# Float32r matmuls of a linear-attention and FFN kernel that read and write their columns in woven blocks of 16, from the halves' ends on

## The chip, the core and the metric

The kernel runs on one core of a Trainium2 chip. The metric is the device time of one launch in microseconds (us); the tables of the trace use nanoseconds (ns) where they say so. The engines are called by the profile's names: PE is TensorE's matmul row, PEld its weight loads, DVE is VectorE, ACT is ScalarE, POOL is GpSimd, SP is the engine whose queue issues the DMAs.

## What is computed

Linear attention without softmax (8 batches, 8 heads, 576 positions, 64 values a head), a root-mean-square norm a head, and a two-layer FFN with SiLU over the 4608 tokens (512 to 2048 to 512), all in float32 accuracy:

```python
kv  = einsum('bhsd,bhse->bhde', k, v)
out = einsum('bhsd,bhde->bhse', q, kv)
out = out / sqrt(mean(out * out, axis=-1, keepdims=True) + 1e-06) * g_norm
x   = out.transpose(0, 2, 1, 3).reshape(B * S, H * D)      # 4608 x 512
h   = x @ w_in                                             # 512 -> 2048
y   = (h / (1 + exp(-h))) @ w_out                          # 2048 -> 512
```

## The kernel before

The tokens are cut into 9 tiles of 512 (t = 0 to 8), the 2048 hidden values into 16 blocks of 128 (f). Every float32 operand of the FFN is kept as two float32r parts, an upper and a lower one, and each product is made of three matmuls (lower by upper, upper by lower, upper by upper) that add into one bank of PSUM. A matmul has a stationary operand of 128 x 128, loaded by a weight load of its own (a LDWEIGHTS for each MATMUL), and a moving operand of 128 partitions by 256 or 512 columns that is read from SBUF while the products are written to PSUM.

Three places make nearly all of TensorE's work:

- `products` (L474), for t = 0 and 1: h of one f, 4 row blocks of x by 3 matmuls, 512 columns each. The stationary side is `wi`, the moving side is `x` (t = 0: the tiles `x0` to `x3`; t = 1: `x_place`).
- `product` (L634), from t = 2 on: h of two f at once by a seven-product scheme. `pair_step` calls it seven times with 6 matmuls of 256 columns each, so 42 a pair step. The moving side lies in `x_operands` (a view of `x_place`) or in `operand4` to `operand6`, the stationary side is `wi` or one of the sums of `wi` blocks, which are read back from DRAM in each pair step (`load_sums`).
- `project` (L505), for all t: y += g @ w_out. The stationary side is a 128-column piece of `gh` or `gl` (the two parts of the SiLU's result), the moving side is a row block of `wo` with 512 columns; 12 matmuls for each f, so 24 a pair step. In the last tile one of the four banks is cut into two halves of 256 columns.

A tile from t = 2 on has 8 pair steps, 56 in all. The attention of later batches (L253 for kv, L288 to L290 for q by kv, 288 columns) is spread between these by hand-written tables of jobs, a few batches ahead of its use. The order on each engine is the order of the code (`manual_schedule`); nothing is reordered by a scheduler.

The SBUF addresses follow from the order of the `const.tile` and pool calls. `SHIFT` (48 columns of 4 bytes) moves `x_operands` inside `x_place` and with it the tiles behind. In the built program, with addresses taken modulo 256 bytes, the tiles `wi`, `wo`, `gh`, `gl` and `x3` start at 224; so does the second tile's x (t = 1). `x0` to `x2`, `x_operands` and `operand4` to `operand6` start at 160, 64 bytes before the weights' place. All starts are thus half a block off a grid of 64 bytes.

Of the kernel before, what the change touches and what calls it, by code (L numbers as in the profile page):

```python
# [8 lines left out]
F32 = mybir.dt.float32  # L9
# [21 lines left out]
def linear_attention_rms_silu_ffn(  # L31
# [22 lines left out]
    nc = tc.nc  # L54
    B, NP, P, S = q.shape
# [3 lines left out]
    TN = 512  # L59
# [5 lines left out]
    const = ctx.enter_context(tc.tile_pool(name="const", bufs=1))  # L65
# [13 lines left out]
        nc.gpsimd.memset(t, 0.0)  # L79
    ident = const.tile([P, P], F32, name="ident", tag="kh", bufs=2)  # L80
    make_identity(nc, ident)
    warm_up = const.tile([P, 1], F32, name="warm_up")
    nc.gpsimd.memset(warm_up, 1.0)
    gcol = const.tile([P, 1], F32, name="gcol")
    both = const.tile([P, P], F32, name="both", tag="kl", bufs=2)
    nc.gpsimd.tensor_copy(out=both, in_=ident)
    for i in range(4):
        nc.gpsimd.tensor_copy(
            out=both[32 * i:32 * i + 32, 32 * (i ^ 1):32 * (i ^ 1) + 32], in_=ident[32 * i:32 * i + 32, 32 * i:32 * i + 32]
        )  # L90
    d_eps = const.tile([P, 1], F32, name="d_eps")
    nc.gpsimd.memset(d_eps, float(D) * EPS)

    def load_g():
        for h in range(P // D):
            nc.sync.dma_start(out=gcol[h * D:(h + 1) * D, :], in_=g_norm.rearrange("(d o) -> d o", o=1))
# [6 lines left out]

    SHIFT = 48
    x_place = const.tile([P, NP * 2 * TN + SHIFT], F32R, name="x_place")
    x_second = x_place[:, :NP * 2 * TN].rearrange("p (c a n) -> p c a n", c=NP, a=2)
    x_operands = x_place[:, SHIFT:].rearrange("p (c a k n) -> p c a k n", c=NP, a=2, k=2)  # L110
    x_first, lates = {}, {}

    def spare(n, shape, dtype, name):
        return const.tile(shape, dtype, name=name, tag=f"spare{n}")

    def late(n, shape, dtype, name):
        if not lates:
            const.tile([P, 64 - SHIFT], F32, name="gap")
        if name not in lates:
            lates[name] = const.tile(shape, dtype, name=name, tag=f"late{n}")  # L120
        return lates[name]

    def x32(c, w):

        return late(c // 2, [P, 2, TN], F32, f"x32_{c // 2}")[:, c % 2, w]
# [14 lines left out]
    def full_tile(kind, f):  # L140
        if kind == "wo":
            t = late(1, [P, 2, NP * P], F32, "wo_full")[:, f % 2]
        else:
            t = tmp.tile([P, S], F32, name="full", tag="tmp")[:, :NP * P]
        fulls[kind, f] = t
        return t
# [54 lines left out]
    def x_part(t, a, c):  # L201

        if t == 1:
            return x_second[:, c, a]
        if c not in x_first:
            kind = {"shape": [P, 2, TN], "dtype": F32R, "name": f"x{c}"}
            x_first[c] = spare(c, **kind) if c < 3 else late(0, **kind)
        return x_first[c][:, a]
# [245 lines left out]
        return calls + 3 * newton(y, u, m)  # L454


    def h_bank():
        return ps_h.tile([P, 512], F32, name="hp", tag="h")

# [10 lines left out]
    def products(hp, t, f, c):  # L470
        w = parts["wi", f]
        fs = slice(c * P, (c + 1) * P)
        for i, (a, b) in enumerate(((0, 1), (1, 0), (0, 0))):
            nc.tensor.matmul(  # L474
                out=hp[:, :TN], lhsT=w[:, a, fs], rhs=x_part(t, b, c),
                start=(c == 0 and i == 0), stop=(c == NP - 1 and i == 2),
            )

# [20 lines left out]
    def project(t, f, gh, gl, bank, n, cs):  # L499
        first, last = order(t)[0], order(t)[-1]  # L500
        w = parts["wo", f]
        ns = slice(n * P, (n + 1) * P)
        bank = bank[:, :cs.stop - cs.start]
        for i, (g, a) in enumerate(((gh, 1), (gh, 0), (gl, 0))):
            nc.tensor.matmul(  # L505
                out=bank, lhsT=g[:, ns], rhs=w[:, a, cs], start=(f == first and i == 0), stop=(f == last and i == 2)
            )
        if f == last:
            ob = tmp.tile([P, S], F32, name="ob", tag="tmp")[:, :cs.stop - cs.start]
            (nc.scalar.copy if n % 2 else nc.vector.tensor_copy)(out=ob, in_=bank)  # L510
            nc.sync.dma_start(out=out[t * TN + n * P:t * TN + (n + 1) * P, cs], in_=ob)
# [9 lines left out]
    def order(t):  # L521

        if t < 2:
            return [(f + t * HF) % NF for f in range(NF)]
        return [f for i in range(HF) for f in (i + HF, i)]
# [69 lines left out]
    def operand(j):  # L595

        if j < 4:
            return x_operands[:, j]
        if j not in operands:
            operands[j] = spare(j - 4, [P, 2, 2, H], F32R, f"operand{j}")  # L600
        return operands[j]
# [26 lines left out]
    def product(m, i, out):  # L628
        j, _, a_of = seven[m]
        x = operand(j)  # L630
        n = 0
        for c in range(2):
            for a, b in ((0, 1), (1, 0), (0, 0)):
                nc.tensor.matmul(  # L634
                    out=out, lhsT=a_of(i, a, c), rhs=x[:, b, c], start=(n == 0), stop=(n == 5)
                )
                n += 1

# [10 lines left out]
    def pair_step(t, i, groups):  # L649
# [5 lines left out]
        def due(n):  # L655
            while n > 0 and groups:
                n -= (groups[0][-1].stop - groups[0][-1].start) / DM
                project(*groups.pop(0))
# [9 lines left out]

        begin(g)
        bank, other = h_bank(), h_bank()  # L670
        u, v = bank[:, :H], bank[:, H:]
        y, z = other[:, :H], other[:, H:]
# [6 lines left out]
        if g == 2 * NF:  # L679
            due(4)  # L680
        product(1, i, u)
        product(2, i, v)
        product(6, i, y)
        product(7, i, z)
        nc.scalar.copy(out=p1, in_=u)  # L685
# [117 lines left out]
    with tc.manual_schedule():  # L803

        first = [FirstPair(c) for c in range(NP)]
        stats = at_bank().rearrange("p (c i j) -> p c i j", i=2, j=8)
        second = plan(1, 3)
        for item in ORDER.split():
            kind, n = item.rstrip("0123456789"), int(item.lstrip("wiopbg") or 0)
# [6 lines left out]
            else:  # L816
                load_block(kind, n)

        idle, kv_bank = h_bank(), h_bank()

        def keep_warm(n, bank=idle):
# [18 lines left out]
        def warm_products(c, *fs):  # L840
            if not warm:
                warm.extend([h_bank(), acc_bank()])
            for f in fs:
                products(warm[f], 0, f, c)
# [115 lines left out]
        for t in range(NT):  # L960
# [7 lines left out]
            for step, f in enumerate(order(t)):  # L968
                g = t * NF + step
                for job in first_jobs.pop(g, ()):  # L970
                    job()
                for item in prepped:
                    split_block(*item, nc.scalar.copy)
                prepped = []
                if t == 0:
                    prepped = [("wi", f + 2)] * (3 <= f + 2 < NF) + [("wo", f)] * (f > 0)
                run(sum((bits(*item) for item in prepped), []), *[call() for call in chains.pop(g, ())])
                if t == 0 and 3 < f + 3 < NF:
                    magnitude("wi", f + 3)
                if t == 0 and f < WARM:  # L980
                    hp = warm[f]
                    products(hp, t, f, NP - 1)
                else:
                    hp = h_bank()
                    for c in range(NP):
                        products(hp, t, f, c)
                pend.append(((t, f, *gate(t, hp)), sums))
                if t == 0 and f + 1 < NF:
                    magnitude("wo", f + 1)
                for job in mid_jobs.pop(g, ()):  # L990
                    job()
                if len(pend) > LAG:
                    item, olds = pend.pop(0)
                    for old in olds:
                        project(*item, *old)
                for job in last_jobs.pop(g, ()):
                    job()
# [4 lines left out]
        for old in sums:  # L1002
            for item, _ in pend:
                project(*item, *old)
# [41 lines left out]
```

## Time and profile before

| | us |
|---|---|
| median of 3 runs (839.11 to 839.32) | 839.13 |
| the profiled execution, own time | 839.63 |
| its span, first to last instruction | 837.8 |
| PE busy in the span | 826.8 (99%) |
| DVE busy | 528.9 (63%) |
| ACT busy | 359.0 (43%) |
| POOL busy | 145.9 (17%) |
| queue of the DMAs, share of 16 engines | 42.4% |

The busy time of PE counts matmuls whose ends are modelled and overlap, so a mean duration (389 ns for 512 columns) is longer than the step from one start to the next. The step is read from the chain of work that ended last: there a piece such as `PE acc L505 x24` with its length gives the time that 24 matmuls in a row took on the path.

### The profile page before, as it was taken

Reading aid. Unit: us, or ns where it says so; the run is one execution under the profiler, and the core shown is the slowest. Engines: PE = TensorE matmul, PEld = TensorE weight load, DVE = VectorE, ACT = ScalarE, POOL = GpSimd, SP = SyncE. Lnnn points to the kernel's source line nnn. Section 1 sums busy time; section 2 is a strip of 40 time slices with the busy share of each in tenths; the row PEclk is TensorE's granted clock in tenths of the full one; section 3 lists DMA queues with packets and bytes.
Section 4 is the critical chain, followed back from the end, with each engine's and each line's share of the span. In section 5 each row is a group of like instructions: output and inputs, shape, how many; then the busy total and the mean of one; then the engine's idle time right before and its main releaser. Section 6 shows DMA issues by size and latency. Waiting matters only on the chain.

```text
span 837.8 us, 14032 instructions
## 1 busy us (share of the span) xinstructions
PE 826.8 (99%) x5454; PEld 734.6 (88%) x5454; DVE 528.9 (63%) x1027; ACT 359.0 (43%) x744; POOL 145.9 (17%) x142
## 2 busy tenths in 40 slices
PE   8999999999999999999999999999999999999998
PEld 7767888888899999998999998999999999999997
DVE  4886875788476567657766667656865664464332
ACT  3766564534453245325532355225532432243222
POOL 2786983423010002000200011001100000000000
PEclk9999999999999999999999999999999999999999
DMA  8879011337343634364424452444423343334331
GB/s 322 313 257 362 4 57 51 136 145 261 122 161 100 215 115 146 101 214 144 165 91 160 163 173 88 158 158 157 151 84 103 106 155 103 105 102 151 100 102 51
DMA packets 42418, 122.55 MB, mean 146 GB/s; under 512 B 4848, under 2 KB 5104, under 8 KB 42352
## 3 DMA queue, kind: packets, MB, share of 16 engines
q1 hardware_dynamic: 42352, 121.65, 42.4%
q8 instruction: 43, 0.70, 0.4%
q14 instruction: 23, 0.19, 0.1%
HBM read 103.81 MB, written 17.83 MB: 145 GB/s over the span
## 4 chain that ended last, share of the span: by engine, by line
PE 94%; DMA 4%; POOL 1%; ACT 0%; issue 0%; SPq 0%
PE acc L505 46%; PE hp L634 33%; PE hp L474 9%; PE at L253 2%; DMA k<-in_k 1%; DMA wo<-in_moe_w_out 1%; DMA early_wi<-in_v 1%; DMA v<-in_v 1%; PE at L289 1%; PE at L288 1%; PE at L290 1%; PE at L505 1%; DMA wi<-in_moe_w_in 1%; PE at L286 1%; POOL wo L191 0%
## 5 line engine op out<-in xcount | busy, mean ns | idle before, releaser
L505 PE MATMUL acc<-wo,gh 128*128 128x512 f32 (+1 forms) x1152 | 354.1, 389 | 0.1
L505 PEld LDWEIGHTS acc<-wo,gh 128*128 128x128 f32 x1152 | 210.3, 188 | 39.7 <-POOL wo L191 0.3
L505 PE MATMUL acc<-wo,gl 128*128 128x512 f32 x576 | 223.0, 387 | 0.5 <-POOL gl L485 0.5
L634 PE MATMUL hp<-x_place,wi 128*128 128x256 f32 x1344 | 167.8, 280 | 0.0
L634 PEld LDWEIGHTS hp<-x_place,wi 128*128 128x128 f32 x1344 | 162.0, 189 | 0.0
L634 PEld LDWEIGHTS hp<-operand,wi 128*128 128x128 f32 x1008 | 126.0, 189 | 3.9
L505 PEld LDWEIGHTS acc<-wo,gl 128*128 128x128 f32 x576 | 108.1, 188 | 23.5 <-POOL gl L485 0.9
L634 PE MATMUL hp<-operand,wi 128*128 128x256 f32 x1008 | 127.5, 281 | 0.0
L275 POOL TENSOR_TENSOR ql<-q,qh 128x576 fp32r<-128x576 f32 x24 | 35.6, 1483 | 376.0 <-ACT qh L274 341.9
L685 ACT COPY wi<-hp 128x256 f32<-128x256 f32 x56 | 20.9, 373 | 140.9 <-PE hp L634 140.9
L643 ACT ACTIVATE gh<-gf 128x512 fp32r<-128x512 f32 x56 | 35.4, 633 | 94.4 <-DVE gf L698 81.6
L643 ACT ACTIVATE gh<-wi 128x512 fp32r<-128x512 f32 x56 | 35.5, 634 | 79.8 <-DVE wi L698 68.0
L686 DVE TENSOR_TENSOR gf<-hp,wi 128x256 f32<-128x256 f32 x28 | 11.9, 425 | 84.8 <-ACT wi L685 84.8
L686 DVE TENSOR_TENSOR wi<-hp,wi 128x256 f32<-128x256 f32 x28 | 11.9, 424 | 84.3 <-ACT wi L685 84.3
L474 PE MATMUL hp<-x,wi 128*128 128x512 f32 x180 | 46.4, 402 | 1.4 <-POOL wi L191 1.4
L474 PE MATMUL hp<-x_place,wi 128*128 128x512 f32 x192 | 46.4, 390 | 0.0
L647 DVE TENSOR_TENSOR gl<-wi,gh 128x512 fp32r<-128x512 f32 x56 | 38.4, 685 | 11.4 <-ACT wi L644 11.4
L687 DVE TENSOR_TENSOR wi<-hp,wi 128x256 f32<-128x256 f32 x56 | 23.8, 425 | 32.3 <-PE hp L634 32.3
L647 DVE TENSOR_TENSOR gl<-gf,gh 128x512 fp32r<-128x512 f32 x56 | 39.0, 696 | 7.3 <-ACT gf L644 7.3
L294 ACT ACTIVATE sq<-at 128x288 f32<-128x288 f32 x56 | 22.9, 410 | 45.6 <-PE at L290 38.9
L474 PEld LDWEIGHTS hp<-x_place,wi 128*128 128x128 f32 x192 | 35.7, 188 | 7.3
L316 DVE SCALAR_TENSOR_TENSOR x<-o,gcol,yT 128x128 f32<-128x128 f32 (+7 forms) x52 | 40.7, 784 | 1.9
(142 smaller groups left out, 1006.8 us busy)
## 6 DMA issues: line engine op xcount, KB each, us to landing
wi<-sums_in_dram SPq DMA_DIRECT2D x112, 512.0 KB, 3.3
out<-ob SPq DMA_DIRECT2D x35, 256.0 KB, 2.4
wi<-in_moe_w_in SPq DMA_DIRECT2D x16, 512.0 KB, 7.8
wo<-in_moe_w_out SPq DMA_DIRECT2D x16, 512.0 KB, 8.9
sums_in_dram<-sum_parts SPq DMA_DIRECT2D x16, 512.0 KB, 2.6
k<-in_k SPq DMA_DIRECT2D x28, 288.0 KB, 5.2
v<-in_v SPq DMA_DIRECT2D x28, 288.0 KB, 5.4
q<-in_q SPq DMA_DIRECT2D x28, 288.0 KB, 4.0
```

The source lines that it names most:

```text
L253: nc.tensor.matmul(out=self.kv[h], lhsT=self.k[rows, c, :], rhs=self.v[rows, c, :], start=(start and r == 0), stop=(stop and r == 4),)
L275: nc.gpsimd.tensor_tensor(out=self.ql, in0=self.q, in1=self.qh.bitcast(F32), op=ALU.subtract)
L294: nc.scalar.activation(out=self.sq[:, self.w], in_=self.ps, func=AF.Square)
L316: nc.vector.scalar_tensor_tensor(out=to, in0=self.o[:, a:e], scalar=gcol, in1=self.yT, op0=ALU.mult, op1=ALU.mult)
L474: nc.tensor.matmul(out=hp[:, :TN], lhsT=w[:, a, fs], rhs=x_part(t, b, c), start=(c == 0 and i == 0), stop=(c == NP - 1 and i == 2),)
L505: nc.tensor.matmul(out=bank, lhsT=g[:, ns], rhs=w[:, a, cs], start=(f == first and i == 0), stop=(f == last and i == 2))
L634: nc.tensor.matmul(out=out, lhsT=a_of(i, a, c), rhs=x[:, b, c], start=(n == 0), stop=(n == 5))
L643: nc.scalar.activation(out=gh, in_=x, func=AF.Silu)
L647: nc.vector.tensor_tensor(out=gl, in0=x, in1=gh.bitcast(F32), op=ALU.subtract)
L685: nc.scalar.copy(out=p1, in_=u)
L686: nc.vector.tensor_tensor(out=c1[:, low], in0=v, in1=p1, op=ALU.add)
L687: nc.vector.tensor_tensor(out=u2, in0=y, in1=p1, op=ALU.add)
```

## The change

The three functions named above pass their moving operand and their output through a new view, `woven`. It cuts the columns into two halves and each half into blocks of 16 columns. The blocks are taken in this order: the last block of the first half, the last block of the second half, the block before it of the first half, and so on down to the halves' first blocks; inside a block the columns still ascend. Moving side and output go through the same view, so each column's result lands where it did, and nothing that reads PSUM or writes the operands changes. The stationary operands, their weight loads, the number of matmuls and their columns are as before. The 288-column matmuls of the attention and the small float32 ones are not woven.

Three placements go with it. `SHIFT` falls from 48 to 32 columns. `warm_up` and `gcol` are allocated behind `both` in place of ahead of it, and a tile of 8 columns named `gap` is added ahead of `x_place`. In the built program `wi`, `wo`, `gh`, `gl`, `x3` and the x of t = 1 then start at 0 modulo 256 bytes, and `x0` to `x2`, `x_operands` and the operands at 128: every start lies on a grid of 64 bytes, so that a block of 16 columns is one block of the grid.

```diff
-    warm_up = const.tile([P, 1], F32, name="warm_up")
-    nc.gpsimd.memset(warm_up, 1.0)
-    gcol = const.tile([P, 1], F32, name="gcol")
     both = const.tile([P, P], F32, name="both", tag="kl", bufs=2)
...
+    warm_up = const.tile([P, 1], F32, name="warm_up")
+    nc.gpsimd.memset(warm_up, 1.0)
+    gcol = const.tile([P, 1], F32, name="gcol")
     d_eps = const.tile([P, 1], F32, name="d_eps")
     nc.gpsimd.memset(d_eps, float(D) * EPS)
+    const.tile([P, 8], F32, name="gap")
...
-    SHIFT = 48
+    SHIFT = 32
...
-            const.tile([P, 64 - SHIFT], F32, name="gap")
+            const.tile([P, 64 - SHIFT], F32, name="gap2")
...
+    def woven(t):
+
+
+        return t.rearrange("p (h k e) -> p k h e", h=2, e=16)[:, ::-1]
+
...
-                out=hp[:, :TN], lhsT=w[:, a, fs], rhs=x_part(t, b, c),
+                out=woven(hp[:, :TN]), lhsT=w[:, a, fs], rhs=woven(x_part(t, b, c)),
...
-                out=bank, lhsT=g[:, ns], rhs=w[:, a, cs], start=(f == first and i == 0), stop=(f == last and i == 2)
+                out=woven(bank), lhsT=g[:, ns], rhs=woven(w[:, a, cs]), start=(f == first and i == 0), stop=(f == last and i == 2)
...
-                    out=out, lhsT=a_of(i, a, c), rhs=x[:, b, c], start=(n == 0), stop=(n == 5)
+                    out=woven(out), lhsT=a_of(i, a, c), rhs=woven(x[:, b, c]), start=(n == 0), stop=(n == 5)
```

No engine's order of instructions changes, only the form of these matmuls. On PE, in a pair step of the first tiles of the seven-product scheme, where `product` (six matmuls a row) is followed by `project`, there stood before (the numbers tell buffers of one tile apart):

```order
L634 MATMUL hp<-operand_2216,wi_2185 128x256 x6
L634 MATMUL hp<-x_place,wi_2185 128x256 x6
L634 MATMUL hp<-x_place,wi_1104 128x256 x6
L634 MATMUL hp<-x_place,wi_2187 128x256 x12
L505 MATMUL acc<-wo_1174,gh 128x512 x2
L505 MATMUL acc<-wo_1174,gl 128x512
```

and in the changed program, at the same place:

```order
L641 MATMUL hp<-operand_2217,wi_2186 128x8x2x16 x6
L641 MATMUL hp<-x_place,wi_2186 128x8x2x16 x6
L641 MATMUL hp<-x_place,wi_1105 128x8x2x16 x6
L641 MATMUL hp<-x_place,wi_2188 128x8x2x16 x12
L512 MATMUL acc<-wo_1175,gh 128x16x2x16 x2
L512 MATMUL acc<-wo_1175,gl 128x16x2x16
```

The rows stand one for one; 256 columns have become 8 times 2 blocks of 16, and 512 have become 16 times 2, so a matmul now reads and writes 16 or 32 short runs.

## Rows read from the trace of the kernel before

**Rows 1.** The profile's page: span, PE's busy time, PE's granted clock in 40 slices.

```profile
span 837.8 us, 14032 instructions
PE 826.8 (99%) x5454; PEld 734.6 (88%) x5454; DVE 528.9 (63%) x1027; ACT 359.0 (43%) x744; POOL 145.9 (17%) x142
PEclk9999999999999999999999999999999999999999
```

**Rows 2.** The chain of waits over the whole span: its shares by line.

```profile
by line: PE acc L505 45.9%; PE hp L634 32.9%; PE hp L474 9.3%; PE at L253 2.2%; DMA k<-in_k 1.0%; DMA wo<-in_moe_w_out 1.0%; DMA early_wi<-in_v 0.9%; DMA v<-in_v 0.8%; PE at L289 0.8%; PE at L288 0.8%; PE at L290 0.8%; PE at L505 0.7%; DMA 
```

**Rows 3.** What PE waited for, seven rows in all: us in total, times, longest.

```profile
PE hp L824 <- POOL ident masks.py:199: 2.0, 1, 2.0
...
PE acc L505 <- POOL gl L485: 0.5, 1, 0.5
```

**Rows 4.** The chain of waits, a pair step of t = 3: start, length (us), piece.

```profile
343.35 4.95 PE hp L634 x42
348.30 5.44 PE acc L505 x24
```

**Rows 5.** The chain of waits in t = 0: two plain float32 matmuls of 288 columns.

```profile
81.22 0.48 PE at L286 x2
```

**Rows 6.** The chain of waits, a stretch with attention matmuls between: start, length, piece.

```profile
411.66 0.13 PE at L290
411.79 2.06 PE hp L634 x18
...
414.26 2.09 PE acc L505 x9
```

**Rows 7.** The chain of waits, t = 0 (first two) and t = 1 (last two).

```profile
84.47 2.79 PE hp L474 x12
87.26 2.73 PE acc L505 x12
...
173.20 2.72 PE hp L474 x12
175.92 2.72 PE acc L505 x12
```

**Rows 8.** The chain of waits, a pair step of the last tile.

```profile
767.12 4.78 PE hp L634 x42
771.90 2.41 PE acc L505 x12
774.31 0.36 PE at L505 x3
```

**Rows 9.** PE's groups by line and shape: count, then busy time and mean of one.

```profile
L505 PE MATMUL acc<-wo,gh 128*128 128x512 f32 x1120 | 347.8, 392 | 0.1
L505 PE MATMUL acc<-wo,gl 128*128 128x512 f32 x560 | 218.5, 390 | 0.5 <-POOL gl L485 0.5
L634 PE MATMUL hp<-x_place,wi 128*128 128x256 f32 x1344 | 167.8, 280 | 0.0
L634 PE MATMUL hp<-operand,wi 128*128 128x256 f32 x1008 | 127.5, 281 | 0.0
L474 PE MATMUL hp<-x_place,wi 128*128 128x512 f32 x192 | 46.4, 390 | 0.0
L474 PE MATMUL hp<-x,wi 128*128 128x512 f32 x180 | 46.4, 402 | 1.4 <-POOL wi L191 1.4
```

**Rows 10.** PE's timeline near the start: start, length, group of matmuls.

```profile
13.95 1.06 PE L341 MATMUL acc<-kvm,early_wi 128*128 128x128 f32 x8
14.84 0.39 PE L824 MATMUL hp<-ident 128*128 128x128 f32 x2
```

**Rows 11.** Stretch, length, busy of PE, PEld, DVE, ACT, POOL; PEclk, DMA, GB/s.

```profile
20.00:120.00 100.00, 95.17 (x555) 75.54 (x555) 79.21 (x131) 63.36 (x128) 78.94 (x79) 1.00 0.53 200
...
400.00:500.00 100.00, 100.00 (x703) 91.02 (x702) 65.50 (x135) 43.45 (x93) 8.96 (x6) 1.00 0.45 151
```

## The prediction

> **What bounds the kernel now.** I read the page first. Its first part says that PE is busy for 826.8 of 837.8 us, and the row of the granted clock says that the throttle never took anything: 2.4 GHz, the higher of the two levels, in all 40 slices [rows 1]. The chain of waits agrees: lines 505, 634 and 474, the three matmuls of the FFN, hold 45.9%, 32.9% and 9.3% of the span [rows 2]. PE's own waits are seven, 2.0 us the longest and 0.5 the shortest [rows 3], under 14 us together whatever lies between. So the time is the number of matmuls times the step from one to the next, and an edit that leaves the order and every other engine alone can only act on that step.
>
> The step is what the reader should look at next, and the chain shows it without the modelled ends. In a quiet pair step 42 matmuls of 256 columns take 4.95 us, 117.9 ns each, and 24 of 512 take 5.44 us, 226.7 ns each [rows 4]. At 2.4 GHz and one column a clock these would be 106.7 and 213.3 ns, so 11.2 and 13.4 ns are lost in each. That one clock a column is the natural rate is seen from the plain float32 matmul: 288 columns take 0.24 us, which is exactly two clocks a column and nothing beside [rows 5]; the loss belongs to the full-rate stream.
>
> Now the same forms elsewhere. Right behind attention matmuls 18 of the 256-column kind take 2.06 us, 114.4 each, while nine of 512 take 2.09 us, 232.2 each [rows 6]. In t = 0, line 474 takes 2.79 us for 12, 232.5 each, with line 505 behind it at 227.5; in t = 1 the same line 474 takes 2.72, 226.7 each [rows 7]. In the last tile the 42 take 4.78 us, 113.8 each [rows 8]. Same line, same columns, same clock, no wait: the step has at least two values for each form. What differs between t = 0 and t = 1 in line 474 is where the moving tile starts against the weights (160 against 224 modulo 256 bytes, then 224 against 224), beside busier neighbours. My reading is that the moving stream and the next weight load, which run side by side, get in each other's way in SBUF, that each encounter costs some clocks, and that the start addresses and what went before decide how many there are.
>
> **The change part by part.** *Orders, counts, other engines.* The counts stay: 2352 matmuls of 256 columns in line 634, 1680 of 512 in line 505, and 372 in line 474 [rows 9], with 96 halves of 256 in line 505 beside. Outputs land where they did, so no reader of PSUM moves. The two tiles allocated later and the 8-column gap cost nothing.
>
> *The weave.* A straight stream walks up through its tile; woven, it stays on one block's place (modulo the halves' distance) for two blocks and walks down at half the speed. If the weight load also walks from its last column down, at half the moving stream's pace, the two keep their distance through the whole load and stop meeting. Whether the load does that is shown by no row. What the rows give is bounds. For 256 columns: at worst nothing is won, 117.2 ns on average (32.9% of 837.8 is 275.6 us over 2352); at best the bare columns, 106.7. Between lies a row with a weight load for each matmul and no straight full-rate stream beside it: eight plain float32 matmuls of 128 columns in 0.89 us (13.95 to 14.84), 111.3 ns each [rows 10]. The load of 128 columns therefore fits into 111.3 ns, and I take 111.3 as the woven step, since this is the nearest row with a load in every step. For 512 columns: most steps are the quiet 226.7 [rows 4, 7], some are 227.5 or 232.2 [rows 6, 7]; I take 227.1 as the mean. Best 213.3. A load takes at most half of such a matmul, so more of the loss should go, but no row shows a 512 below 226.7; I take the middle of 226.7 and 213.3, 220.0.
>
> *The sum.* Line 634: 2352 x 5.9 ns = 13.9 us. Line 505: 1680 x 7.1 = 11.9 us, and the 96 halves, at 120 ns (0.36 us for 3 [rows 8]), brought to about 114, 0.6 us. Line 474: t = 1, 192 x 6.7 = 1.3 us; t = 0, 180 x 12.5 = 2.3 us. Together 30.0 us. In t = 0 the cover is thin: DVE, ACT and POOL are busy 79, 63 and 79 of 100 us [rows 11], so of what lines 474 and 505 win there (2.3 and 192 x 7.5 = 1.4 us) I give half back to waits on POOL, 1.9 us. From t = 2 on nothing is near: DVE at 65.5 of 100 us, DMA at 0.45 of its share [rows 11]; four percent less PE time raises that to 68, and PE waits for nothing there. So 28.1 us.
>
> *Alignment.* Every start moves by 32 bytes or so, for weights and for the 144 unwoven 288-column matmuls too. Their step is 0.13 or 0.14 us [rows 6]; a change of 5 ns either way is 0.7 us. I take nothing.
>
> The Trainium skill speaks against the reading: "TensorE: Matmul & The Clock Gate", in its Part 2, gives PE two independent SBUF read ports, so that the next weights' load takes nothing from the running matmul. By that rule the weave would change nothing; [rows 4, 6, 7], with two steps for one form, do not settle it, since a neighbour's write could also be the cause. The same page's isolated step, columns over 2.4 GHz and about 2.5 ns, would be 109.2 and 215.8 ns here, an estimate from that page by which the sum would be some 19 us for line 634 and 19 for line 505.
>
> **The rivals.** *Only the unlucky phases go.* The weave keeps the streams in the better of the two states that the trace already has: 113.8 ns [rows 8] and 226.7. That is 2352 x 3.4 = 8.0 us, 1680 x 0.4 = 0.7, and 180 x 5.8 = 1.0 in t = 0: 9.7 us, 829.9. For it: no row of 2352 in line 634 shows a group below 113.8. Against: the better states are those of straight streams, in which the two still cross.
>
> *No change.* The loss is not an encounter with the weight load but belongs to the full-rate float32r stream: then 839.6, within 1 us. For it: 226.7 is twice 113.3, so the loss is nearly in proportion to the columns in the better states, as it would be if the stream itself lost one clock in 16, and a load of fixed size would not give that. Against: the other states, which are not in proportion (117.9 and 226.7; 114.4 and 232.2). The rule of the two ports is this rival.
>
> *Slower: each run costs.* A woven matmul reads and writes 16 or 32 runs in place of one, and a jump of address on either side may cost a clock. At one clock of 0.417 ns, 16 runs are 6.7 ns and 32 are 13.3: 2352 x 6.7 + 2052 x 13.3 = 43.0 us. If my gain is there too, the end is 811.5 + 43.0 = 854.5; if not, 882.6. It decides from 0.37 ns a run (5.9 over 16) for 256 columns, and from 0.22 ns (7.1 over 32) for 512: less than one clock. For it: no row of before has a stream with jumps, so nothing bounds it. Against: each run is 64 bytes and now starts on a grid of 64. The Trainium skill's "PSUM — Partial Sum Buffer", under Specifications, says that any non-contiguous access pattern slows matmuls significantly; that rule is this rival. [...]
>
> *More than forecast.* All loss goes: 2352 x 10.5 + 1680 x 13.8 + 192 x 13.4 + 180 x 19.2, 53.9 us, 785.7. I see it as the floor.
>
> **How the numbers follow.** The profiled execution took 839.63 us, 1.8 more than its span; the median is 839.13. 839.6 less 28.1 is 811.5, and on the median's scale 811.0; I predict 811. Chances: forecast and what lies about it (788 to 822) 0.46, only the phases 0.22 (822 to 837), no change 0.10, each run costs 0.20, below 788 0.02. A difference of 0.2%, 1.7 us, is about what a measurement of this kernel can tell from no change; so faster 0.70, same 0.10, slower 0.20. The range runs from 788, near the floor, over the phases and no change to 843, where a run's cost has just passed break-even; what it leaves out is most of the slower case and the floor. The likeliest case by itself is 788 to 822.
>
> **What would show it.** In the chain of waits of the changed kernel the pieces of 42 and of 24 matmuls give the answer: about 4.67 us and 5.28 us for the forecast, 4.78 and 5.44 for the phases alone, 4.95 and 5.44 for no change, over 5.2 and 5.6 for a cost a run. The 12 of line 474 in t = 0 should come down from 2.79 most. Weight loads, counts and granted clock should be as before, and PE's waits beyond t = 0 still absent; were new waits on DVE or ACT to stand in the rows from t = 2 on, my cover would be wrong. If one form gains and the other doesn't, then the relative start of the two streams, which differs between line 505 (0) and line 634 (128 bytes), decides and not the weave alone.

## The result and the profile after

The changed kernel takes 847.14 us (median of 3 runs, 846.99 to 847.26) against 839.13 before: a ratio of 1.0095 with a 95% interval of 1.0072 to 1.0118. It is slower by about 1%, where 811 us was forecast, and outside the range. Its lines 481, 512 and 641 are lines 474, 505 and 634 of before.

The page of the changed kernel, the parts that answer to [rows 1]:

```profile
span 845.2 us, 14053 instructions
PE 835.0 (99%) x5454; PEld 733.5 (87%) x5454; DVE 529.4 (63%) x1027; ACT 359.3 (43%) x744; POOL 145.3 (17%) x142
PEclk9999999999999999999999999999999999999999
```

The same 5454 matmuls, the higher clock level (2.4 GHz) in all 40 slices, the other engines within 0.6 us of before. PE's waits are seven again. The first and the last row of that view (us in total, times, longest):

```profile
PE hp L831 <- POOL ident masks.py:199: 2.0, 1, 2.0
...
PE hp L255 <- DMA early_wo<-in_v: 0.2, 1, 0.2
```

The longest is still 2.0 us, and the seven add up to 7.0 us where they were 7.7, so no wait makes the 8 us. What grew is the step. The chain of waits by line (share of the span), to be held against [rows 2]:

```profile
by line: PE acc L512 46.4%; PE hp L641 32.5%; PE hp L481 9.3%; PE at L255 2.2%; DMA wo<-in_moe_w_out 1.0%; DMA k<-in_k 1.0%; PE at L292 0.8%; PE at L290 0.8%; PE at L291 0.7%; DMA v<-in_v 0.7%; DMA wi<-in_moe_w_in 0.7%; PE at L512 0.7%; DMA
```

Multiplied by the spans, `project` went from 384.5 to 392.2 us, `product` from 275.6 to 274.7, `products` from 77.9 to 78.6: together 7.5, and the span grew by 7.4. (A share is rounded to 0.1%, some 0.4 us either way.) So the whole loss lies in the 512-column matmuls.

The chain in a quiet pair step of t = 4 (start, length in us, piece), to be held against [rows 4]:

```profile
440.86 5.61 PE acc L512 x24
446.46 4.90 PE hp L641 x42
```

24 matmuls of 512 columns take 5.60 us where they took 5.44: 233.3 ns a step in place of 226.7. 42 of 256 columns take 4.90 where they took 4.95: 116.7 in place of 117.9. One form loses 6.6 ns, the other wins 1.2.

The chain elsewhere: t = 0 and t = 1 (to be held against [rows 7]), behind attention matmuls ([rows 6]), and in the last tile ([rows 8]):

```profile
83.84 2.77 PE hp L481 x12
86.61 2.80 PE acc L512 x12
...
173.90 2.80 PE hp L481 x12
...
415.00 2.10 PE hp L641 x18
...
417.49 2.12 PE acc L512 x9
...
773.25 4.90 PE hp L641 x42
```

Line 481 wins 1.7 ns a matmul in t = 0 (2.79 to 2.77 for 12), where three of its four moving tiles start 128 bytes before the weights' place and `x3` at it, and loses 6.6 in t = 1, where both start at the same place modulo 256 bytes (2.72 to 2.80). In the last tile `product` loses what it had: 4.78 becomes 4.90. The woven 256-column step is 116.7 everywhere, quiet or disturbed; the straight one was 117.9, 114.4 or 113.8.

### The profile page after: what moved, and what is told of

Read it like the earlier page. It is cut to its first block, busy times and chain, and to the rows that moved or that the text cites. A ratio compares the mean times of both kernels' runs of the same rounds, so it can differ in the third digit from the quotient of the medians.

```text
span 845.2 us, 14053 instructions
## 1 busy us (share of the span) xinstructions
PE 835.0 (99%) x5454; PEld 733.5 (87%) x5454; DVE 529.4 (63%) x1027; ACT 359.3 (43%) x744; POOL 145.3 (17%) x142
## 4 chain that ended last, share of the span: by engine, by line
PE 94%; DMA 4%; POOL 1%; ACT 0%; issue 0%; SPq 0%
PE acc L512 46%; PE hp L641 32%; PE hp L481 9%; PE at L255 2%; DMA wo<-in_moe_w_out 1%; DMA k<-in_k 1%; PE at L292 1%; PE at L290 1%; PE at L291 1%; DMA v<-in_v 1%; DMA wi<-in_moe_w_in 1%; PE at L512 1%; DMA early_wi<-in_v 1%; PE at L288 1%; POOL wo L193 0%
## 5 line engine op out<-in xcount | busy, mean ns | idle before, releaser
L512 PE MATMUL acc<-wo,gh 128*128 128x512 f32 (+1 forms) x1152 | 359.0, 392 | 0.1
L512 PE MATMUL acc<-wo,gl 128*128 128x512 f32 x576 | 225.5, 391 | 0.5 <-POOL gl L492 0.5
L693 DVE TENSOR_TENSOR wi<-hp,wi 128x256 f32<-128x256 f32 x28 | 11.9, 425 | 87.1 <-ACT wi L692 87.1
L693 DVE TENSOR_TENSOR gf<-hp,wi 128x256 f32<-128x256 f32 x28 | 11.9, 425 | 87.0 <-ACT wi L692 87.0
```

Source lines behind the costliest of these rows:

```text
L512: nc.tensor.matmul(out=woven(bank), lhsT=g[:, ns], rhs=woven(w[:, a, cs]), start=(f == first and i == 0), stop=(f == last and i == 2))
L693: nc.vector.tensor_tensor(out=c1[:, low], in0=v, in1=p1, op=ALU.add)
```

## The experiments

Below, the **distance** is how far the weights' start lies behind the moving operand's start, modulo 256 bytes. Three theories were tried. *Phase*: the step of a matmul with a weight load beside it is set by the distance and by the order in which the moving stream visits its columns. *Placement*: the new start addresses alone do it, and the weave is beside the point. *Each run costs*: a jump of address has a price, whatever the addresses.

### The parts of the change, one by one

**New starts, straight streams.** The changed kernel with

```diff
-        return t.rearrange("p (h k e) -> p k h e", h=2, e=16)[:, ::-1]
+        return t
```

> The new placement (SHIFT 32, the gap tile, all starts on the grid of 64 bytes) with straight columns on both sides, as before. Theory 'phase' (the step is set by how the moving stream and the next weight load meet, and the weave breaks the good meeting of the 512-column matmuls): 512 columns stay at 226 to 227 ns in quiet stretches, the time is 836 to 841 us. Theory 'each run costs' (about 6.6 ns for 32 runs): the same, 839 or a little less. Theory 'placement' (the grid of 64 bytes, not the weave, costs): 847 us, with 512 columns at 233 ns.

Measured: 846.72 us (846.31 to 846.95), ratio 1.0089 [1.0074, 1.0104]. Its chain by line, and a quiet pair step:

```profile
by line: PE acc L512 45.6%; PE hp L641 33.3%; PE hp L481 9.2%; PE at L255 2.2%; DMA wo<-in_moe_w_out 1.0%; DMA wi<-in_moe_w_in 0.9%; DMA k<-in_k 0.9%; PE at L290 0.8%; PE at L291 0.8%; DMA early_wo<-in_k 0.8%; PE at L292 0.8%; PE at L512 0.
...
445.04 5.04 PE hp L641 x42
450.07 5.48 PE acc L512 x24
```

The time is as placement expected, but in the other form; the 836 to 841 of phase missed. `project` stays near its old step (228.3 ns; distance 0 as before), and `product`, whose distance went from 64 to 128 bytes, rises from 117.9 to 120.0. By shares of the span, in us:

| | before | new starts, straight | new starts, woven (the change) |
|---|---|---|---|
| `project` | 384.5 | 385.3 | 392.2 |
| `product` | 275.6 | 281.4 | 274.7 |
| `products` | 77.9 | 77.7 | 78.6 |
| span | 837.8 | 845.0 | 845.2 |

The change is thus two edits: the new starts cost 7.2 us of the span, most of it in `product`; the weave gives 6.7 back there and takes 6.9 in `project`. The split depends on the order: taken first, the weave costs 10.1 us, and the new starts then give 2.1 back, as the next run shows.

**The weave, old starts.** The kernel before, with `woven` and its six uses and nothing else of the diff.

> The weave in all three places, with the placement of before (SHIFT 48, starts 32 bytes off the grid of 64, so each block of 16 columns lies over two blocks of the grid). Theory 'each run costs': 847 us, as after, or more, since a run then touches two blocks. Theory 'phase': some other time, 840 to 870, since the relative starts are others. Theory 'placement': 839.

Measured: 849.23 (849.17 to 849.47), ratio 1.0120 [1.0103, 1.0136]. A quiet pair step:

```profile
441.47 5.60 PE acc L510 x24
447.07 4.94 PE hp L639 x42
```

At distance 0 the woven 512-column step is 233.3 with the old starts too, so half a block off the grid of 64 or on it is the same. At distance 64 the 256-column step gains almost nothing (117.6). The time is far from the 839 of placement; phase (840 to 870) and a cost a run (847 or more) both allow it.

**The weave in `product` alone.** The changed kernel with straight operands in the other two:

```diff
-                out=woven(hp[:, :TN]), lhsT=w[:, a, fs], rhs=woven(x_part(t, b, c)),
+                out=hp[:, :TN], lhsT=w[:, a, fs], rhs=x_part(t, b, c),
...
-                out=woven(bank), lhsT=g[:, ns], rhs=woven(w[:, a, cs]), start=(f == first and i == 0), stop=(f == last and i == 2)
+                out=bank, lhsT=g[:, ns], rhs=w[:, a, cs], start=(f == first and i == 0), stop=(f == last and i == 2)
```

> Of the changed kernel the weave in the 256-column product alone; project and products read and write straight. Theory 'phase': the 512-column matmuls return to 226.7 ns and the 256-column ones stay near 116.6, so about 847 less 2050 x 6 ns, 833 to 836 us. Theory 'each run costs': 256 columns carry 16 runs, so half the cost of a 512; 512 return to 226.7, 836 to 840. Theory 'placement': 847.

Measured: 837.75 (837.64 to 838.03), ratio 0.9984 [0.9975, 0.9993], a gain of 1.4 us.

```profile
441.70 4.90 PE hp L641 x42
446.60 5.44 PE acc L512 x24
```

The good half of the change alone: 116.7 where it was 117.9, and 226.7 kept. Woven columns can be cheaper than straight ones, though 16 runs stand in place of one. The time missed the 833 to 836 of phase and lies in the range of each run costs, so it does not decide between them: the sum took 6 ns from every 512-column matmul, but behind attention matmuls the weave had cost less (nine in 2.12 us, straight 2.09 [rows 6]).

### The step by itself

**Matmuls alone.** A program of nothing but float32r matmuls with a weight load each (the model is left out; a copy of an input to the output runs beside the first three groups): groups of 48 with 512 columns and 72 with 256, at eight distances, 0 to 448 bytes in steps of 64 (names end in a to h).

```diff
+    "long_woven": (512, woven, woven, 0),
+    "long_woven_out": (512, in_turn, woven, 0),
...
+                            out=write(bank[:cols, :n]), lhsT=weights[:, w0:w0 + cols], rhs=read(moving[:, m0:m0 + n]),
```

> Not the model's computation: matmuls alone, in rows of 48 (512 columns) or 72 (256 columns), nothing else running beside, for each way of reading and writing (straight, straight 32 bytes off the grid, woven down, woven up, blocks down without the interleave, woven on the moving side alone, woven on the output side alone) and for eight distances of the weights' start from the moving start (letters a to h: 0 to 448 bytes in steps of 64); 'light' rows load only 32 weight columns; what is written to the output is a copy of an input. Theory 'phase': the step changes with the letter by 4 to 8 ns, for straight and woven alike, the output side alone changes nothing, and light rows come near 213 and 107 ns. Theory 'each run costs': woven is 6 to 7 ns above straight at 512 and about 3 at 256 for every letter, light rows too. No dependence on the letter at all would be against 'phase'.

The chain of waits of that program (start, length of the whole group in us, group); `up` is the weave with ascending blocks, `out` weaves only the output, `light` loads 32 weight columns in place of 128:

```profile
32.44 11.16 PE long_straight_c L96 x48
43.60 10.99 PE long_straight_d L96 x48
54.60 10.90 PE long_straight_e L96 x48
65.50 11.20 PE long_straight_f L96 x48
...
187.34 11.19 PE long_woven_a L96 x48
198.54 11.36 PE long_woven_b L96 x48
209.89 10.96 PE long_woven_c L96 x48
...
276.29 11.52 PE long_woven_up_a L96 x48
...
547.75 10.93 PE long_woven_out_a L96 x48
...
647.40 11.13 PE long_light_b L96 x48
...
821.65 8.48 PE short_straight_b L96 x72
830.13 8.55 PE short_straight_c L96 x72
...
966.65 8.40 PE short_woven_c L96 x72
...
1163.20 8.16 PE short_light_b L96 x72
```

Divided by the counts, in ns:

| distance, bytes | 0 | 64 | 128 | 192 |
|---|---|---|---|---|
| 512 straight | 227.1 | 233.3 | 232.5 | 229.0 |
| 512 woven, descending | 233.1 | 236.7 | 228.3 | 228.3 |
| 512 woven, ascending | 240.0 | 240.0 | 240.0 | 240.0 |
| 256 straight | 120.0 | 117.8 | 118.8 | 117.8 |
| 256 woven, descending | 119.9 | 117.4 | 116.7 | 116.7 |

Distances e to h repeat a to d, so the period is 256 bytes (e stands for a in the straight row of 512, since the program's start lies in a). One form, one clock, nothing else at work from the fourth group on, and the step moves by 6 ns with the distance alone: this shows that *phase* is real. It holds most of the case's numbers: `project` at 0 goes from 227.1 to 233.1, `product` at 64 straight is 117.8, at 128 woven 116.7. One it does not hold: at 128 straight it has 118.8, where the kernel with the new starts took 120.0. Moving all starts by 32 bytes changed no group by more than 0.02 us (the first aside), the output's weave is free (10.93 and 11.20 woven, 10.90 and 11.20 straight) while the moving side's alone gives the woven steps (11.20 and 11.36), and ascending blocks cost the same at every distance. The *placement* theory in its plain form and *each run costs* both fail here: the same 32 runs take 228.3 to 240.0 ns.

With a load of 32 columns the 512-column step is 231.9 at b and 230.4 to 231.9 at all eight distances: nearly no dependence, but not the 213 that was expected. The 256-column step does fall, to 113.3, but not to 107.

**The distance mended in the changed kernel.** A tile that nothing uses moves `gh` and `gl`, the weights of `project`, by 128 bytes:

```diff
+    small.tile([P, 32], F32, name="pad", bufs=1)
```

> The changed kernel with a pad of 128 bytes ahead of gh and gl, so that line 505's stationary tiles start 128 bytes (modulo 256) from wo, as line 634's already do, and not at the same place. Theory 'phase', by the table of matmuls alone (woven 512 at distance 0: 233.3 ns, at 128: 228.3; measured in the changed kernel 233 at distance 0): 1680 x 5 ns = 8 us less than the changed kernel, 839 us, with the 24 of a pair step at 5.48 us instead of 5.60. Theory 'each run costs': no change, 847.

Measured: 839.47 (839.12 to 839.72), ratio 1.0003 [0.9993, 1.0012].

```profile
442.70 4.90 PE hp L642 x42
447.60 5.49 PE acc L513 x24
```

The time is as phase expected. The weave is as it was, every run of it, and 7.7 of the 8.0 us are gone: the woven step of `project` falls from 233.3 to 228.8 (228.3 in the table). This settles that the loss is the weave *at distance 0*.

**The distance spoiled in the kernel before.** The same with 16 columns: `gh` and `gl` come to distance 64, no weave anywhere.

```diff
+    small.tile([P, 16], F32, name="pad", bufs=1)
```

> The kernel of before (straight) with a pad of 64 bytes ahead of gh and gl alone, so line 505 has distance 64 where it had 0. Theory 'phase', by the table (straight 512: 226.7 at 0, 233.4 at 64): 1680 x 6.7 ns less the few stretches that are disturbed already, 9 to 11 us more, 848 to 850. Theory that only the order of the columns matters: 839.

Measured: 845.95 (845.86 to 846.31), ratio 1.0081 [1.0066, 1.0096], 2 us less than expected. Two pair steps, and one of the last tile:

```profile
440.33 5.60 PE acc L506 x24
445.92 4.78 PE hp L635 x42
...
456.29 4.95 PE hp L635 x42
...
782.62 4.95 PE hp L635 x42
```

`project` rises to 233.3 as the table has it for a straight stream at 64. The miss is a surprise in `product`, whose operands the pad does not move: in about every second pair step from t = 2 to 7 it takes 4.78 us, the value that before only the last tile showed [rows 8]; in the last tile, with the halves of 256 columns ahead as before, it now takes 4.95. One form at one distance has two steps. Since nothing of its own changed, what ran ahead of it chooses, but not by its form alone.

**The weave ascending.** The changed kernel with

```diff
-        return t.rearrange("p (h k e) -> p k h e", h=2, e=16)[:, ::-1]
+        return t.rearrange("p (h k e) -> p k h e", h=2, e=16)
```

> The changed kernel with the weave going up from the halves' beginnings (the same 32 or 16 runs, the same placement). Theory 'phase', by the table (woven up: 240.0 and 120.0 at every distance): 2050 x 7 ns and 2350 x 3.4 ns more than the changed kernel, 22 us, 869 us. Theory 'each run costs': the number of runs is the same, so 847.

Measured: 869.60 (869.42 to 869.76), ratio 1.0362 [1.0344, 1.0379].

```profile
447.10 5.04 PE hp L641 x42
452.14 5.75 PE acc L512 x24
```

120.0 and 239.6 ns, as in the table. The runs are as many and as long as in the changed kernel; turning them round costs 22.5 us. *Each run costs* cannot hold that.

**Other orders, alone.** The program of matmuls again, with other views of the moving operand, and other column counts at distance 0 (the model is left out).

```diff
+    "long_one_block": (512, one_block, rows_of_16, 128, straight),
+    "long_weave_by_sixtyfour": (512, weave(2, 64), weave(2, 64), 128, straight),
+    "n_two": (320, straight, straight, 128, straight),
+    "n_three": (384, straight, straight, 128, straight),
```

> Not the model's computation: rows of matmuls alone, as in the first table, at four distances (a to d: 0, 64, 128, 192 bytes), for other orders of the moving columns: wholly backwards, one block of 16 read again and again, weaves with blocks of 8, 32 and 64 or of four parts, blocks of 64 downwards, every second weight column, and straight matmuls of 128, 320, 384 and 448 columns; what is written to the output is a copy of an input. Theory 'phase' (two walks that meet in four places of 64 bytes): one block read again meets the load at most in one place, so it is the best, near 218 for 512; a weave by 8 is like straight backwards; if the loss were the stream's alone (one clock in 16), one block read again would still take 226.7 and the step would grow by 17/16 of the columns.

Some groups of its chain (long names are cut to their last letters; `step_two` loads every second weight column):

```profile
52.47 8.56 PE long_one_block_b L104 x36
...
182.08 8.20 PE ong_weave_by_sixtyfour_a L104 x36
190.28 8.40 PE ong_weave_by_sixtyfour_b L104 x36
...
316.71 8.39 PE long_weights_step_two_a L104 x36
325.10 8.28 PE long_weights_step_two_b L104 x36
...
382.19 5.28 PE n_two_b L104 x36
...
398.02 6.27 PE n_three_a L104 x36
```

The guess of 218 ns for a stream that stays on one block fell: it takes 237.8 to 242.2, more than a straight one. So did the one that a weave by 8 is like straight backwards: 240.0 against 233.3 at 64, 128 and 192. A weave by blocks of 64 columns (256 bytes) is the straight stream again: 227.8 at distance 0 and 233.3 at 64. Blocks of 64 taken downwards give the same (227.2 and 233.3). So jumps and direction are free as long as they are of 256 bytes; what counts is the order within 256 bytes. It is not the order of the four 64-byte places alone: at 128, wholly backwards takes 233.3 and blocks of 16 downwards, which visit these places in the same order, 236.7. The halves lie 512 or 1024 bytes apart, whole multiples of 256, so the change's weave visits each place twice in a row and walks down, and that is where it differs from a straight stream.

And 384 columns take 174.2 ns, 14.2 above their bare 160.0 (one clock a column); at this distance 256 lose 13.3, 320 lose 14.4, 448 lose 16.4 and 512 lose 13.8. At the best distance of the four 320, 384 and 448 columns take 146.7, 173.3 and 200.0, and the quiet 512 took 226.7: 26.7 ns for each 64 columns, which is one clock a column, and 13.3 beside. This loss is one of a matmul, not of a column; only 256 columns have a state that loses 6.7 (113.3).

**The weave by 64 in the kernel.** The kernel before with `woven` in all three places and

```diff
+        return t.rearrange("p (h k e) -> p k h e", h=2, e=64)[:, ::-1]
```

> The placement of before, all three places woven as in the change, but with blocks of 64 columns (256 bytes) in place of 16: 8 or 4 runs in turn from the halves' ends on, so each next 64 bytes still lie in the next of the four places modulo 256. Theory 'phase' in the form that the second table gave it (only the order of these four places counts; jumps and direction beyond 256 bytes are free; 226.7, 233.4, 232.1, 228.9 as for straight columns): the time of before, 838.5 to 840. Theory 'each run costs' (6.6 ns for 32 runs, so 1.6 for 8): 839 + 2050 x 1.6 + 2350 x 0.8 ns, 844.

Measured: 839.30 (838.92 to 839.74), ratio 1.0001 [0.9992, 1.0010].

```profile
442.59 4.95 PE hp L639 x42
447.54 5.44 PE acc L510 x24
```

As phase expected: the very steps of [rows 4], with 4 or 8 runs in each matmul.

**Finer distances, alone.** Sixteen distances 16 bytes apart (a to p), straight, woven and with half a load.

```diff
+            for d in range(16):
```

> Not the model's computation: rows of matmuls alone as in the other tables (an input is copied to the output), for straight and woven columns and for loads of 64 weight columns, at sixteen distances of 16 bytes (letters a to p). Theory 'phase': the steps at distances between the multiples of 64 lie between their neighbours or equal one of them; if places of 64 bytes are the unit, distances within one place give equal steps wherever the moving side starts on the grid. Half a load: the loss over 213.3 and 106.7 ns falls with the load if it were proportional to it; in the first table the light load of 32 columns gave 231.7 at 512, so by that it doesn't.

```profile
165.64 5.44 PE short_straight_e L90 x48
...
267.13 8.52 PE long_woven_e L90 x36
275.65 8.16 PE long_woven_f L90 x36
...
411.81 5.44 PE short_woven_i L90 x48
```

`e` is distance 64 with 256 straight columns: 113.3 ns here, 117.8 in the first program of matmuls alone. A whole group of 48 or 72 keeps one value or the other, so these are two steady states. The woven 256 has them too: at 128 (`i`) and 192 it takes 113.3 here, as at every distance from 80 to 192, and 116.7 in the first program. The woven 512 reaches 226.7 at one distance of sixteen (80 bytes) and no less.

What phase expected of the distances between the multiples of 64 fell: at 64, 80 and 96 the woven 512 takes 236.7, 226.7 and 228.3, so distances within 64 bytes are not equal, and 80 lies below both neighbours of the first table. Half a load takes 226.7 to 235.6 ns for 512 columns and 113.3 to 120.0 for 256: the loss does not fall with the load, and the distance still counts. Of all groups of 512 columns with a full load none is under 226.7, of 256 none under 113.3.

### A kernel faster than both

The two steps of `product` gave an idea: in [rows 8] its 4.78 us stand behind a `project` whose bank was cut into two halves of 256 columns. The kernel before with the last bank of every pair step of t = 2 to 7 cut in the same way, all straight:

```diff
-        for i, (g, a) in enumerate(((gh, 1), (gh, 0), (gl, 0))):
+        cut = 1 < t < NT - 1 and n == 3 and f < HF
+        for j in range(2) if cut else (None,):
+            part = slice(None) if j is None else (low, high)[j]
+            for i, (g, a) in enumerate(((gh, 1), (gh, 0), (gl, 0))):
...
-                out=bank, lhsT=g[:, ns], rhs=w[:, a, cs], start=(f == first and i == 0), stop=(f == last and i == 2)
+                    out=bank[:, part], lhsT=g[:, ns], rhs=w[:, a, cs][:, part], start=(f == first and i == 0),
+                    stop=(f == last and i == 2 and j != 0),
```

> The kernel of before, straight, but in t = 2 to 7 the last bank of each pair step (n = 3 of the second f) is projected as two halves of 256 columns, so the 42 matmuls of line 634 follow 256-column ones, as they do in the last tile, where they take 4.78 us and not 4.95. Theory 'phase' with a memory (the same distances have two stable steps, 113.3 and 117.8 ns, and what runs ahead chooses): 4.78 us in the pair steps, 0.17 us less each, against 0.04 for the cut and 0.03 for the six 512-column matmuls that follow it at 231 to 235: about 3 us less in all, 835 to 837. Rival (the last tile is faster for another reason): 4.95 stays, and the cut adds 2 to 3 us, 841 to 842.

Measured: 833.87 (833.78 to 833.95), ratio 0.9936 [0.9919, 0.9953].

```profile
440.75 4.78 PE hp L638 x42
445.53 5.49 PE acc L508 x27
451.02 4.78 PE hp L638 x42
```

27 matmuls in place of 24 cost 0.05 us a pair step, and `product` gives back 0.17: 48 pair steps by 0.12 are 5.8 us, of which 5.4 were measured, more than the 3 expected. It does 144 matmuls more than the kernel before and is faster. The rival, that the last tile is faster for another reason, fell. Why matmuls of 256 columns ahead leave the following ones in the lower state was not found, and with `project` at distance 64 they do not (4.95 in the last tile above).

## Why the prediction was wrong, point by point

**What bounds the kernel: right.** The time is the count times the step, and nothing else moved: clock, waits and engines are as before, and the three lines hold the whole difference.

**That start and history set the step: right, and then not used.** [Rows 6 to 8] were read as the moving stream and the next load meeting, more or less often by their starts. The dependence on distance was shown by the matmuls alone, that on history by the two states and the cut bank. But the sum gave the woven step one value for every distance. The forecast's own last sentence, that one form gaining and the other not would mean the relative start, is what came.

**The step that failed: the weave.** It was assumed, with no row for it, that a stream going down at half speed keeps its distance from the load and stops meeting it. The weave changes the order in which the 64-byte places are read, and what that does hangs on the distance: 227.1 to 233.1 ns at 0 (`project`), 118.8 to 116.7 at 128 (`product`). So line 505 was forecast at -11.9 us and came at +7.7; line 474 at t = 1 at -1.3 and came at 192 x 6.6 = +1.3, at t = 0 at -2.3 and came at 180 x 1.7 = -0.3.

**The sizes.** 111.3 and 220.0 ns were out of reach: with a full load no group of the matmuls alone is under 113.3 and 226.7, straight or woven, at any distance. The 111.3 of [rows 10] came from matmuls of 128 columns, where the load seems to set the step: 128 float32r columns, 53.3 ns bare, take 6.65 us for 60, 110.8 each. The row bounds the load, not a 256-column matmul beside one. (At the two clocks a column of [rows 5] the plain matmuls of [rows 10] would need 106.7 for their columns alone.) For line 634, -13.9 us was forecast and -0.9 came, since its quiet steps won 1.2 ns and its better ones [rows 6, 8] lost 2.3 and 2.9.

**"Alignment. I take nothing": the second miss.** The grid of 64 is indeed worth nothing (groups 32 bytes off it are the same). But the placement also moved line 634 from distance 64 to 128, as the start addresses told, and with straight streams the new starts cost 7.2 us, most of it in that line. That a new distance has a price was there to be read in [rows 7], where line 474 takes 232.5 ns with three of its four moving tiles at 64 and 226.7 at 0; none was put on it.

**The rivals.** *Only the unlucky phases go* named the floors rightly, 113.8 and 226.7. Alone, the woven 256 columns reached 113.3 in one program and 116.7 in another; in the changed kernel every unbroken group of 42 on the chain took 4.90 us, and `project` was at its floor already. *No change* rested on a loss of one clock in 16; the best steps lose 13.3 ns for 320, 384, 448 and 512 columns alike. These steps also show the one clock a column, which the two clocks of the plain matmul [rows 5] did not. The Trainium skill's rule of two independent read ports ("TensorE: Matmul & The Clock Gate", Part 2), which stood beside that rival, does not agree with the matmuls alone: with nothing else at work, moving the weights' start takes 48 matmuls from 10.90 to 11.20 us. *Each run costs* had the right sign by luck: the cause is another. The ascending weave (22.5 us more with as many runs), the pad (7.7 less with every run) and the weave by 64 refute the mechanism. So does the woven output, which also speaks against the rule of the Trainium skill's "PSUM — Partial Sum Buffer", Specifications, for runs of 16 columns: 10.93 against 10.90 us.

**What stays open.** What the moving stream meets was not settled. The load takes part: with 32 columns of it the 512-column step is nearly independent of the distance, and a load of every second weight column takes 233.1 and 230.0 ns at 0 and 64 in place of 227.1 and 233.3. But a smaller load does not make that step shorter, and one block read again and again is slow with 32 columns too (8.51 to 8.77 us for 36). Whether the rest belongs to the moving read or to having a load at all is not shown, since no matmul ran without one. Nor is it known what in the matmuls ahead chooses between 113.3 and 117.8, nor why `product`, straight at 128, takes 120.0 in the kernel and 118.8 alone.

## What to carry to other kernels

When a loss depends on relative addresses, an edit that moves addresses and changes the access order is two edits: price each at the distance of every user, since the same weave won at one distance and lost at another. Before costing a new form at a bound taken from another form, measure the form alone over all relative starts; here one program of matmuls gave the table that the forecast lacked. And look in the trace for the better state that the kernel already reaches somewhere: what ran ahead of it there was worth more (5.4 us) than the best of the reorderings (1.4).

## What the runs showed of the hardware that was not expected

- The step of a matmul with its own weight load depends on the distance between the two starts modulo 256 bytes: 227.1, 233.3, 232.5 and 229.0 ns for 512 straight columns at 0, 64, 128 and 192.
- Reading order matters only within 256 bytes: by blocks of 64 columns it is free (227.8), while the same 64-byte place twice in a row, ascending, takes 240.0 at every distance, and one place read throughout 237.8 to 242.2.
- 256 columns have two steady steps at one distance, 113.3 and 117.8 ns. Six matmuls of half width ahead brought the lower one in the kernel before (4.78 us for 42), but not with `project` at distance 64 (4.95).
- The best steps of 320 to 512 columns with a load each are one clock a column and 13.3 ns.
- Runs of 16 columns on the output side cost nothing that shows.
